# Windowed attention and two MLP layers on one core: block 0's first two steps in column parts, softmax normalising by head, and weight loads behind the third unit's q and k

## The chip, the core and the metric

The kernel runs on one core of a Trainium2 chip. A core has TensorE (PE, matrix multiply), VectorE (DVE), ScalarE (ACT), GpSimd (POOL) and SyncE (SP, which issues all of this kernel's transfers here). The metric is the device time of one execution in microseconds (us); smaller is better.

## What is computed

Attention of 8 heads over 4 batches of 576 tokens with head size 64, then two MLP layers of width 512 and 2048 on all 2304 tokens, in float32.

```python
scores = q @ k.T / 8          # heads 0-3: keys 0..31 positions back
                              # heads 4-7: keys 0..127 positions back, every fourth
scores = where(mask, scores, -1e9); scores -= max
attn = exp(scores); attn /= sum(attn) + 1e-9
x = (attn @ v) with the heads side by side        # 2304 x 512
h = x @ w_in;  g = h * sigmoid(1.702 * h);  x = g @ w_out
h = x @ w_in2; g = relu(h) ** 2;            y = g @ w_out2
```

## The kernel before

**Attention** is cut into units: a batch, a pair of heads and half of the 576 positions, 8 units a batch, 32 in all (`attend`, L407). For heads 4 to 7 the positions are sorted by their remainder by four, so half `u` holds remainders 2u and 2u + 1. A unit works on three blocks of 96 queries by 128 keys for each of its two heads: 12 score matmuls into two PSUM banks (`scores`, L448); six VectorE instructions that add the mask and find the row maxima (L470); six ScalarE exponentials with row sums (L477); a guard and a reciprocal (L491, L494); six instructions that scale 96x128 by the reciprocal, each on ScalarE or VectorE (`normalise`, L496, through `scaled`, L244 and L246); six transposes on TensorE (L527), or from batch 2 on by VectorE (L512); copies into the tile `pt`, of which there is one; 12 value matmuls (L546); then the result is split into a high and a low part, `x` (L240 or L238, and L562). In batch 0 the transposes and values, and the scores of every second unit, use the four PSUM banks of class "o". Units three and six of batch 0 keep their scores in `g` tiles.

**Layers** run over blocks of up to 512 tokens (`BLOCKS1`, `BLOCKS2`). A block has 16 steps `f`, one for each 128 of the 2048 inner columns (`step`, L572). A step does 12 "hidden" matmuls (L590 to L592: four slices `k` of 128 inputs, each as high x high, high x low, low x high), the nonlinearity on ScalarE and VectorE (L613 and L616, or L623 and L626), the split of `g` into `gh` and `gl`, and 12 "output" matmuls (L657 to L659) into four "o" banks that a block holds from its first step to its last. Slice `k` of the inputs is a pair of heads. A block's tokens are ordered by remainder by four, 144 (`ROW`) to a remainder and batch: block 0 has remainders 0, 1 and 2 and 80 tokens of remainder 3 of batch 0. So each of its slices needs both halves of a pair of heads, and block 0 needs all eight units of batch 0, in the order pairs (0, 0, 1, 1, 2, 3, 2, 3), halves (0, 1, 0, 1, 0, 0, 1, 1).

**Weights** come as 64 tiles of 512 KB in eight-byte numbers, and are turned into a high and a low float32r tile by four instructions: a cast of the upper bits, `c` (L238 or L240), a join on VectorE (L314), a high part (L238 or L240) and a low part on VectorE (L249). There are three raw buffers and two `c` buffers. Step `f` needs two weights, (f, 0) for its hidden and (f, 1) for its output matmuls.

**Order.** Every instruction is a task of a planner written into the kernel (`Schedule`, L63). A task has one engine or several to choose from, a cost on each, a due time (`want`), the tasks that it follows and the buffers that it takes. `emit` (L119) again and again takes the task that can start first by its own clock, on ties the one due first, and issues it; so the order on each engine is fixed when the kernel is built. Where GpSimd is among the choices, VectorE is charged 3 us extra for tasks due before 160 us (`spare`). Tasks of GpSimd, and those of VectorE marked `port`, are not placed at the same time. A transfer is ready as soon as its buffer is. While TensorE would idle in batch 0 the planner puts in matmuls on zeros ("warm", L718), which hold one of the two "h" banks until all of batch 0's values are done. Units of batches 1 to 3 are spread between the steps of the first blocks.

Of the kernel before, what the change touches and what calls it, by code (L numbers as in the profile page):

```python
# [15 lines left out]
ALU = mybir.AluOpType  # L16
# [3 lines left out]
P = 128  # L20
# [3 lines left out]
NPAIR = H // 2  # L24
KD = DM // P
KF = DFF // P
WIN = 32
QB = 96
NBLK = 3
# [5 lines left out]
ROW = S // 4  # L35
# [5 lines left out]
A1 = 1.0  # L41
BAND_FROM = 2
W2_GAP = 4.0
WARM = 256
MASK_AT = -9.0
LEAD = (12.0, 8.0, 5.0)
# [21 lines left out]
class Schedule:  # L68
# [18 lines left out]
    def buffer(self, cls):  # L87
        return {"cls": cls, "held": False, "left": 0, "end": 0.0}

    def task(self, engine, cost, want, fn, after=(), bufs=(), port=False):  # L90


        many = isinstance(engine, tuple)
        t = {
            "ways": dict(zip(engine, cost)) if many else {engine: cost}, "many": many,
            "want": want, "fn": fn, "bufs": bufs, "port": port,
            "left": 0, "ready": [], "next": [], "n": len(self.tasks), "end": None,
        }
        for a in after:
            a["next"].append(t)  # L100
            t["left"] += 1
        for b in bufs:
            b["left"] += 1
        self.tasks.append(t)
        return t
# [7 lines left out]

    def open(self, t):
        for e, cost in t["ways"].items():
            ready = max([end + (self.SAME[e] if d == e else self.HOP[d]) for end, d in t["ready"]], default=0.0)
            self.opened[e].append((t, ready, cost, self.spare(t, e)))

    def emit(self):  # L119
# [69 lines left out]
def attention_mlp_mlp(  # L189
# [9 lines left out]
    V, A, G, T = nc.vector, nc.scalar, nc.gpsimd, nc.tensor  # L199
# [89 lines left out]
    def weights(layer, f, part, want):  # L289


        m = {}
        raw_b, c_b, w_b = buffer("raw"), buffer("c"), buffer(f"w{f}_{part}")
        name = f"{f}_{part}"

        def load():

            m["raw"] = wst.tile([P, DM, 2], U32, tag="raw", bufs=RAW_BUFS, name="raw")
            nc.sync.dma_start(
                m["raw"].rearrange("p n t -> p (n t)").bitcast(U16)[:, 0:4 * DM - 1],  # L300
                (w1, w2)[layer][f, part].bitcast(U16)[:, 1:4 * DM],
            )

        def top(e):

            m["c"] = tops[top_count[0] % C_BUFS]
            top_count[0] += 1
            halves = m["raw"].rearrange("p n t -> p (n t)").bitcast(BF16).rearrange("p (n t) -> p n t", t=4)[:, :, 2]  # L310
            copy(e, m["c"].bitcast(F16).rearrange("p (n t) -> p n t", t=2)[:, :, 1], halves)

        def join():
            V.scalar_tensor_tensor(  # L314
                out=m["raw"][:, :, 0], in0=m["raw"][:, :, 0], scalar=13, in1=m["c"],
                op0=ALU.logical_shift_right, op1=ALU.bitwise_or,
            )

        def value():
            return m["raw"][:, :, 0].bitcast(F32)  # L320

        def high_part(e):
            wh[layer, f, part] = wpool.tile([P, DM], F32R, tag="wh" + name, name="wh" + name)
            copy(e, wh[layer, f, part], value())

        def low_part(e):
            wl[layer, f, part] = wpool.tile([P, DM], F32R, tag="wl" + name, name="wl" + name)
            minus(e, wl[layer, f, part], value(), wh[layer, f, part])

        t = task("dma", 1.456, want - LEAD[0], load, (), [raw_b])  # L330
        t = task(("act", "dve"), (0.67, 0.38), want - LEAD[1], top, [t] + tops_zero, [raw_b, c_b], True)
        t = task("dve", 0.602, want - LEAD[1], join, [t], [raw_b, c_b], True)
        hi = task(*copies(DM), want - LEAD[2], high_part, [t], [raw_b, w_b], True)
        lo = task(*pairs(DM), want - LEAD[2], low_part, [hi], [raw_b, w_b], True)
        split_task[layer, f, part] = [hi, lo]
        wbuf[layer, f, part] = w_b
# [70 lines left out]
    def attend(b, p, u, want, start, turn_pe, i):  # L407
# [85 lines left out]
        def recip():  # L493
            V.reciprocal(out=m["st"][:, 2], in_=m["st"][:, 1])  # L494

        def normalise(e, j, i):  # L496
            scaled(e, m["sm", j][:, i], m["sm", j][:, i], m["st"][:, 2, j, i:i + 1])

        es = head(0) + head(1)
        t = task("dve", 0.08, want, guard, es, [st_b], True)  # L500
        t = task("dve", 0.12, want, recip, [t], [st_b], True)
        for j in range(2):
            normal.append([
                task(
                    ("act", "dve"), (0.292, 0.196), want, lambda e, j=j, i=i: normalise(e, j, i),
                    [t], [st_b, sm_bs[j]], True,
                )
                for i in range(NBLK)
            ])

        def band(a, e):
# [41 lines left out]
        for n, w, src_, dst_ in x_pieces(b, p, u):  # L553
            if n not in x_buf:
                x_buf[n] = buffer(x_place[n])

            def to_hi(e, n=n, src_=src_, dst_=dst_):
                copy(e, dst_(x_tile(n), 0), src_(m["o"]))

            def to_lo(n=n, src_=src_, dst_=dst_):  # L560
                x = x_tile(n)
                V.tensor_tensor(out=dst_(x, 1), in0=src_(m["o"]), in1=dst_(x, 0), op=ALU.subtract)  # L562

            t = task(("act", "dve"), (0.07 + w / 1340, dve1(w)), want, to_hi, [pv], [pv_b, x_buf[n]])
            t2 = task("dve", dve1(w), want, to_lo, [t], [pv_b, x_buf[n]])
            x_done.setdefault((n, p), []).extend([t, t2])


    stored = {}
    close = {}  # L570

    def step(layer, blk, f, want, a=0, z=None):  # L572

        z = z or blk["n"]
        n = z - a
# [6 lines left out]
        for k in range(KD):  # L582

            def hidden(k=k):
                if k == 0:
                    m["h"] = bank("h", "h")
                w_hi, w_lo = wh[layer, f, 0], wl[layer, f, 0]
                x = blk["x"]()
                out, ks = m["h"][:, 0:n], slice(k * P, (k + 1) * P)
                T.matmul(out, w_hi[:, ks], x[:, 0, k, a:z], start=(k == 0), stop=False)  # L590
                T.matmul(out, w_hi[:, ks], x[:, 1, k, a:z], start=False, stop=False)  # L591
                T.matmul(out, w_lo[:, ks], x[:, 0, k, a:z], start=False, stop=(k == KD - 1))  # L592

            before = [t] if t else [chain["hidden"]] if "hidden" in chain else []
            t = task(
                "pe", 3 * pe, want + k * 3 * pe, hidden,
                split_task[layer, f, 0] + blk["ready"](k) + before, [h_b, x_b, w_in],
            )
            if k == 0:
                chain["hidden"] = t  # L600
# [37 lines left out]

        hi = task(*copies(n), want, high_part, [last], [g_b, gh_b], True)
        lo = task(*pairs(n), want, low_part, [hi], [g_b, gh_b, gl_b], True)  # L640
        if f == 0:
            blk["o_buf"] = [buffer("o") for _ in range(KD)]
            blk["o"], blk["ost_buf"], blk["evacs"] = {}, {}, {}
        for d in range(KD):


            extra = a > 0
            more_b = [buffer("sshh"[d])] if extra else []

            def project(d=d, extra=extra):  # L650
                if f == 0:
                    blk["o"][d] = bank("o", "o")
                w_hi, w_lo = wh[layer, f, 1], wl[layer, f, 1]
                if extra:
                    m["more", d] = bank("sshh"[d], "more")[:, 0:n]
                out, ds_ = m["more", d] if extra else blk["o"][d][:, a:z], slice(d * P, (d + 1) * P)
                T.matmul(out, w_hi[:, ds_], m["gh"], start=(f == 0 or extra), stop=False)  # L657
                T.matmul(out, w_lo[:, ds_], m["gh"], start=False, stop=False)  # L658
                T.matmul(out, w_hi[:, ds_], m["gl"], start=False, stop=(f == KF - 1))  # L659

            t = task(
                "pe", 3 * pe, want + (12 + 3 * d) * pe, project,
                split_task[layer, f, 1] + [hi, lo], [gh_b, gl_b, w_out, blk["o_buf"][d]] + more_b,
            )
            if f == KF - 1:

                cls = "raw2" if n < blk["n"] and d > 1 else "ost"
# [92 lines left out]
    def step_len(size):  # L760
        return 24 * mm(size)
# [6 lines left out]
    for n, size in enumerate(sizes1):  # L768
        blk = {
            "i": n, "n": size, "c0": sum(sizes1[:n]), "buf": x_buf[n],  # L770
            "x": lambda n=n: x_t[n], "ready": lambda k, n=n: x_done[n, k],
        }
        lb = ((begin + begin2)[n + 1] - begin[n]) / KF
        for f in range(KF):
            step(0, blk, f, begin[n] + lb * f)


# [10 lines left out]
    for n, size in enumerate(BLOCKS2):  # L788
# [2 lines left out]
        cls = ("xx", "x0", "x1", "x2", "xx")[n]  # L791
        blk = {"i": n, "n": size, "c0": c0, "buf": buffer(cls), "done": {}}
        blk["x"] = lambda blk=blk: blk["tile"]
        blk["ready"] = lambda k, blk=blk: blk["done"][k]
        need = [
            i for i, size1 in enumerate(sizes1)
            if sum(sizes1[:i]) < c0 + size and sum(sizes1[:i]) + size1 > c0
# [23 lines left out]
        for f in range(KF):  # L821
            w = want + step_len(size) * f
            if n == len(BLOCKS2) - 1 and f == KF - 1 and size == 512:

                step(1, blk, f, w, 0, size // 2)
                step(1, blk, f, w + step_len(size // 2), size // 2, size)
            else:
                step(1, blk, f, w)

# [87 lines left out]
```

## Time and profile before

| | us |
|---|---|
| median of 3 runs | 891.55 |
| lowest, highest | 890.49, 893.07 |
| the profiled execution | 889.98 |
| its span from first to last instruction | 888.0 |
| TensorE busy in it | 873.6 (98%) |
| VectorE busy | 436.2 (49%) |
| ScalarE busy | 388.3 (44%) |
| GpSimd busy | 2.1 (0%) |

The rows of the profile name an engine, a line of the kernel, an operation, the tile that it writes and the one that it reads, partitions by elements, and how many there are. Busy time is the sum of instructions' durations, which overlap on one engine where it works on several; the distance between starts in the chain of waits tells what one costs in a full queue. "Idle before" names what ended the engine's last wait. The chain of waits goes back from the last instruction and names at each step what released it.

### The profile page before, as it was taken

Reading aid. Unit: us, or ns where it says so; the run is one execution under the profiler, and the core shown is the slowest. Engines: PE = TensorE matmul, PEld = TensorE weight load, DVE = VectorE, ACT = ScalarE, POOL = GpSimd, SP = SyncE. Lnnn points to the kernel's source line nnn. Section 1 sums busy time; section 2 is a strip of 40 time slices with the busy share of each in tenths; the row PEclk is TensorE's granted clock in tenths of the full one; section 3 lists DMA queues with packets and bytes.
Section 4 is the critical chain, followed back from the end, with each engine's and each line's share of the span. In section 5 each row is a group of like instructions: output and inputs, shape, how many; then the busy total and the mean of one; then the engine's idle time right before and its main releaser. Section 6 shows DMA issues by size and latency. Waiting matters only on the chain.

```text
span 888.0 us, 12713 instructions
## 1 busy us (share of the span) xinstructions
PE 873.6 (98%) x4761; PEld 719.9 (81%) x4761; DVE 436.2 (49%) x1231; ACT 388.3 (44%) x1035; POOL 2.1 (0%) x9
## 2 busy tenths in 40 slices
PE   7899999999999999999999999999999999999997
PEld 5677777777799988888877788888889988888886
DVE  6888774666668734446778422422232222222223
ACT  7999976543455523335546322222232322232222
POOL 0000000000000000000000000000000000000000
PEclk9999999999999999999999999999999999999999
DMA  7466752111121100216465200000000000000001
GB/s 253 143 216 205 229 195 87 45 38 42 47 89 58 43 15 1 84 41 220 166 195 186 93 1 1 35 25 1 1 24 25 9 16 1 1 30 18 1 1 48
DMA packets 27533, 64.98 MB, mean 73 GB/s; under 512 B 3056, under 2 KB 9200, under 8 KB 27472
## 3 DMA queue, kind: packets, MB, share of 16 engines
q1 hardware_dynamic: 27472, 64.18, 22.0%
q8 instruction: 37, 0.61, 0.3%
q14 instruction: 24, 0.20, 0.1%
HBM read 54.73 MB, written 9.44 MB: 72 GB/s over the span
## 4 chain that ended last, share of the span: by engine, by line
PE 85%; DVE 5%; DMA 4%; ACT 4%; issue 1%; SPq 0%; DVEq 0%; ACTq 0%
PE o L657 14%; PE h L590 14%; PE o L659 14%; PE o L658 13%; PE h L592 13%; PE h L591 13%; DMA raw<-in_w 3%; PE s L454 2%; PE pv L546 2%; DVE wl L249 1%; ACT sm L477 1%; ACT sm L244 1%; DVE raw L314 1%; PE tp L527 1%; ACT c L238 1%
## 5 line engine op out<-in xcount | busy, mean ns | idle before, releaser
L657 PE MATMUL o<-gh,wh 128*128 128x512 f32 (+1 forms) x640 | 237.3, 371 | 0.3 <-ACT gh L238 0.3
L659 PE MATMUL o<-gl,wh 128*128 128x512 f32 (+1 forms) x640 | 235.7, 368 | 0.6 <-DVE gl L249 0.4
L658 PE MATMUL o<-gh,wl 128*128 128x512 f32 (+1 forms) x640 | 235.1, 367 | 0.0
L590 PE MATMUL h<-x,wh 128*128 128x512 f32 (+1 forms) x512 | 190.9, 373 | 1.9 <-DVE g L616 0.8
L592 PE MATMUL h<-x,wl 128*128 128x512 f32 (+1 forms) x512 | 186.2, 364 | 0.5 <-DVE wl L249 0.5
L591 PE MATMUL h<-x,wh 128*128 128x512 f32 (+1 forms) x512 | 186.0, 363 | 0.1
L626 DVE TENSOR_TENSOR g<-g 128x512 f32<-128x512 f32 (+1 forms) x81 | 51.2, 632 | 217.6 <-ACT g L623 216.8
L623 ACT ACTIVATE g<-h 128x512 f32<-128x512 f32 (+1 forms) x81 | 44.5, 550 | 222.9 <-PE h L592 222.8
L657 PEld LDWEIGHTS o<-gh,wh 128*128 128x128 f32 x640 | 120.6, 188 | 22.8 <-ACT gh L238 1.2
L659 PEld LDWEIGHTS o<-gl,wh 128*128 128x128 f32 x640 | 120.6, 188 | 22.6 <-DVE gl L249 2.6
L658 PEld LDWEIGHTS o<-gh,wl 128*128 128x128 f32 x640 | 120.6, 188 | 19.5
L249 DVE TENSOR_TENSOR gl<-g,gh 128x512 fp32r<-128x512 f32 (+1 forms) x161 | 101.7, 634 | 64.8 <-ACT gh L238 62.2
L238 ACT CAST gh<-g 128x512 fp32r<-128x512 f32 (+1 forms) x149 | 85.9, 580 | 87.3 <-DVE g L626 54.4
L590 PEld LDWEIGHTS h<-x,wh 128*128 128x128 f32 x512 | 96.8, 189 | 20.5 <-DVE g L616 1.8
L592 PEld LDWEIGHTS h<-x,wl 128*128 128x128 f32 x512 | 96.6, 189 | 16.5 <-DVE wl L249 1.2
L591 PEld LDWEIGHTS h<-x,wh 128*128 128x128 f32 x512 | 96.7, 189 | 14.3 <-DVE x L562 0.8
L477 ACT ACTIVATE sm<-sm,st 96x128 f32<-96x128 f32 x180 | 70.1, 393 | 23.6 <-DVE st L470 23.5
L613 ACT ACTIVATE g<-h 128x512 f32<-128x512 f32 (+1 forms) x80 | 43.9, 552 | 77.6 <-PE h L592 75.8
L616 DVE SCALAR_TENSOR_TENSOR g<-g,h 128x512 f32<-128x512 f32 (+1 forms) x80 | 50.2, 629 | 54.1 <-ACT g L613 53.4
L314 DVE SCALAR_TENSOR_TENSOR raw<-raw,c 128x512 uint32<-128x512 uint32 x64 | 44.1, 691 | 21.3 <-ACT c L238 21.0
L238 ACT CAST c<-raw 128x512 f16<-128x512 bf16 x54 | 42.0, 781 | 27.3 <-DMA raw<-in_w 23.7
L470 DVE CUSTOM_DVE_ANT_0 sm<-s,mask_sb 96x128 f32<-96x128 f32 x180 | 41.6, 281 | 24.8 <-PE s L454 23.7
(66 smaller groups left out, 712.8 us busy)
## 6 DMA issues: line engine op xcount, KB each, us to landing
raw<-in_w SPq DMA_DIRECT2D x64, 511.8 KB, 4.0
qk<-in_qkv SPq DMA_DIRECT2D x32, 304.0 KB, 2.9
v<-in_qkv SPq DMA_DIRECT2D x32, 192.0 KB, 2.6
x2d<-ost SPq DMA_DIRECT2D x16, 256.0 KB, 2.2
raw<-x2d SPq DMA_DIRECT2D x16, 256.0 KB, 2.8
out_T<-ost SPq DMA_DIRECT2D x14, 256.0 KB, 2.0
x2d<-ost SPq DMA_DIRECT2D x4, 128.0 KB, 1.7
raw<-x2d SPq DMA_DIRECT2D x4, 128.0 KB, 2.2
```

Source lines behind the costliest of these rows:

```text
L238: A.copy(out, in_)
L249: by_name[e].tensor_tensor(out=out, in0=a, in1=b, op=ALU.subtract)
L314: V.scalar_tensor_tensor(out=m["raw"][:, :, 0], in0=m["raw"][:, :, 0], scalar=13, in1=m["c"], op0=ALU.logical_shift_right, op1=ALU.bitwise_or,
L477: A.activation(out=m["sm", j][:, i], in_=m["sm", j][:, i], func=AF.Exp, bias=m["st"][:, 0, j, i:i + 1], scale=-1.0, accum_out=m["st"][:, 1 ...
L590: T.matmul(out, w_hi[:, ks], x[:, 0, k, a:z], start=(k == 0), stop=False)
L591: T.matmul(out, w_hi[:, ks], x[:, 1, k, a:z], start=False, stop=False)
L592: T.matmul(out, w_lo[:, ks], x[:, 0, k, a:z], start=False, stop=(k == KD - 1))
L616: V.scalar_tensor_tensor(out=g(), in0=g(), scalar=1.0, in1=h(), op0=ALU.add, op1=ALU.mult)
L626: by_name[e].tensor_tensor(out=g(), in0=g(), in1=g(), op=ALU.mult)
L657: T.matmul(out, w_hi[:, ds_], m["gh"], start=(f == 0 or extra), stop=False)
L658: T.matmul(out, w_lo[:, ds_], m["gh"], start=False, stop=False)
L659: T.matmul(out, w_hi[:, ds_], m["gl"], start=False, stop=(f == KF - 1))
```

## The change

Three things. First, a unit's scaling by the reciprocal becomes one task for each head in place of three: one multiplication of 96x384 by the reciprocals, spread along the keys, on GpSimd or VectorE in batch 0, and in later batches the same on VectorE or three instructions on ScalarE. Second, the loads of weights are not ready before 7 us of the planner's clock; before, they were ready at once. Third, the first two steps of block 0 are made in two parts each, columns 0 to 288 (remainders 0 and 1) of both steps, then columns 288 to 512 of both. The first part waits for both halves of pairs 0 and 1 and for the first half alone of pairs 2 and 3, so for the first six units; the second part waits for all. Both parts write the same four "o" banks; only the very first matmul into a bank starts it afresh. Output matmuls of the same part and bank keep the order of steps. Elsewhere in the kernel a step that was already cut in two (the last one) works as before.

```diff
+HALVES = 2
+FIRST = 2 * ROW
+RAW_FROM = 7
...
-    def task(self, engine, cost, want, fn, after=(), bufs=(), port=False):
+    def task(self, engine, cost, want, fn, after=(), bufs=(), port=False, since=0.0):
...
-            ready = max([end + (self.SAME[e] if d == e else self.HOP[d]) for end, d in t["ready"]], default=0.0)
+            ready = max([end + (self.SAME[e] if d == e else self.HOP[d]) for end, d in t["ready"]], default=t["since"])
...
-        t = task("dma", 1.456, want - LEAD[0], load, (), [raw_b])
+        t = task("dma", 1.456, want - LEAD[0], load, (), [raw_b], since=RAW_FROM)
...
-        def normalise(e, j, i):
-            scaled(e, m["sm", j][:, i], m["sm", j][:, i], m["st"][:, 2, j, i:i + 1])
+        def normalise(e, j):
+            if e == "act":
+                for n in range(NBLK):
+                    scaled(e, m["sm", j][:, n], m["sm", j][:, n], m["st"][:, 2, j, n:n + 1])
+            else:
+                by_name[e].tensor_tensor(
+                    out=m["sm", j], in0=m["sm", j],
+                    in1=m["st"][:, 2, j].rearrange("q (i o) -> q i o", o=1).to_broadcast([QB, NBLK, P]),
+                    op=ALU.mult,
+                )
...
         for j in range(2):
+            ways = {"pool": 0.98, "dve": 0.47} if start else {"act": 0.9, "dve": 0.47}
             normal.append([
                 task(
-                    ("act", "dve"), (0.292, 0.196), want, lambda e, j=j, i=i: normalise(e, j, i),
+                    tuple(ways), tuple(ways.values()), want, lambda e, j=j: normalise(e, j),
                     [t], [st_b, sm_bs[j]], True,
                 )
-                for i in range(NBLK)
             ])
...
-            x_done.setdefault((n, p), []).extend([t, t2])
+            x_done.setdefault((n, p, u), []).extend([t, t2])
...
-    def step(layer, blk, f, want, a=0, z=None):
+    def step(layer, blk, f, want, a=0, z=None, own=False):
...
-                split_task[layer, f, 0] + blk["ready"](k) + before, [h_b, x_b, w_in],
+                split_task[layer, f, 0] + blk["ready"](k, z) + before, [h_b, x_b, w_in],
...
-            extra = a > 0
+            extra = own
...
-                if f == 0:
+                if f == 0 and a == 0:
                     blk["o"][d] = bank("o", "o")
...
-                T.matmul(out, w_hi[:, ds_], m["gh"], start=(f == 0 or extra), stop=False)
+                T.matmul(out, w_hi[:, ds_], m["gh"], start=(f == 0 and a == 0 or extra), stop=False)
...
-                split_task[layer, f, 1] + [hi, lo], [gh_b, gl_b, w_out, blk["o_buf"][d]] + more_b,
+                split_task[layer, f, 1] + [hi, lo] + blk.setdefault(("last", a, d), []), [gh_b, gl_b, w_out, blk["o_buf"][d]] + more_b,
             )
+            blk["last", a, d] = [t]
...
-            "x": lambda n=n: x_t[n], "ready": lambda k, n=n: x_done[n, k],
+            "x": lambda n=n: x_t[n],
+            "ready": lambda k, z, n=n: [
+                t for u in range(2) if z > FIRST or k < NPAIR // 2 or u == 0 for t in x_done.get((n, k, u), [])
+            ],
...
-        for f in range(KF):
+        cut = HALVES if n == 0 else 0
+        for i in range(2 * cut):
+            f = i % cut
+            w = begin[n] + (step_len(FIRST) * f if i < cut else step_len(FIRST) * cut + step_len(size - FIRST) * f)
+            step(0, blk, f, w, *((0, FIRST) if i < cut else (FIRST, size)))
+        for f in range(cut, KF):
             step(0, blk, f, begin[n] + lb * f)

```

## Rows read from the trace of the kernel before

**Rows 1.** Stretches: us, busy time and instructions of each engine, clock, DMA share, GB/s

```profile
10.00:47.50 37.50, 33.17 (x305) 22.62 (x303) 31.59 (x174) 37.10 (x155) 0.00 (x0) 1.00 0.57 177
47.50:120.00 72.50, 72.49 (x410) 56.34 (x411) 59.27 (x159) 66.09 (x179) 0.00 (x0) 1.00 0.65 215
120.00:860.00 740.00, 738.20 (x3888) 616.67 (x3887) 333.69 (x856) 273.26 (x673) 0.58 (x1) 1.00 0.16 53
```

**Rows 2.** Order of time, VectorE: start us, us, engine, line, operation

```profile
42.34 0.52 DVE L562 TENSOR_TENSOR x<-pv,x 128x224 fp32r<-128x224 f32 x2
```

**Rows 3.** Order of time, TensorE near 46.5 us; in brackets the idle time before

```profile
46.55 0.50 PE L590 MATMUL h<-x,wh 128*128 128x512 f32 x1 [0.81 <-ACT wh L238]
```

**Rows 4.** Chain of waits, TensorE full: start us, us, line

```profile
59.80 0.83 PE s L454 x12
...
66.99 0.55 PE tp L527 x6
...
68.96 0.65 PE pv L546 x12
...
865.93 0.23 PE h L590
...
874.77 0.11 PE h L590
...
877.64 0.23 PE o L657
```

**Rows 5.** Groups by line and form, 0 to 47.5 us: busy us, mean ns, idle before

```profile
L454 PE MATMUL s<-qk 64*96 64x128 f32 x120 | 11.5, 314 | 3.2 <-DMA qk<-in_qkv 2.2 <-DVE st L470 0.8 <-DVE pt L240 0.2
...
L546 PE MATMUL pv<-pt,v 128*64 128x96 f32 x108 | 8.0, 256 | 0.7 <-ACT pt L238 0.5
```

**Rows 6.** Normalising, 0 to 47.5 us: groups, then order of time, then the chain

```profile
L244 ACT ACTIVATE sm<-sm,st 96x128 f32<-96x128 f32 x28 | 9.0, 400 | 0.2 <-DVE st L494 0.2
...
L246 DVE TENSOR_SCALAR sm<-sm,st 96x128 f32<-96x128 f32 x14 | 3.3, 277 | 0.0
...
L246 DVE TENSOR_SCALAR g<-g,st 96x128 f32<-96x128 f32 x8 | 1.7, 278 | 0.0
...
L244 ACT ACTIVATE g<-g,st 96x128 f32<-96x128 f32 x4 | 1.4, 393 | 0.0
...
41.88 1.89 ACT L244 ACTIVATE sm<-sm,st 96x128 f32<-96x128 f32 x6
...
19.03 0.79 DVE g L246 x4
```

**Rows 7.** Groups of GpSimd, whole span

```profile
L285 POOL MEMSET c<- 128x512 uint32 x2 | 1.0, 524 | 0.3 <-POOLq L900 0.3
...
masks.py:199 POOL TENSOR_SCALAR_AFFINE_SELECT ident<-ident 96x96 f32<-96x96 f32 x1 | 0.3, 262 | 0.1
```

**Rows 8.** Order of time: SyncE's queue and TensorE, and a piece of the chain

```profile
3.52 1.43 SPq L299 DMA_DIRECT2D raw<-in_w  x3
5.35 2.73 SPq L420 DMA_DIRECT2D qk<-in_qkv  x2
...
12.21 0.46 PE L454 MATMUL s<-qk 64*96 64x128 f32 x4 [0.15 <-DMA qk<-in_qkv]
...
2.10 3.94 DMA qk<-in_qkv
```

**Rows 9.** Chain of waits in the block of 256 columns

```profile
295.73 0.34 DVE g L616
...
296.09 0.41 ACT gh L238
```

**Rows 10.** Groups that split weights, 0 to 47.5 us

```profile
L238 ACT CAST c<-raw 128x512 f16<-128x512 bf16 x4 | 3.1, 778 | 0.0
...
L314 DVE SCALAR_TENSOR_TENSOR raw<-raw,c 128x512 uint32<-128x512 uint32 x4 | 2.8, 689 | 1.1 <-ACT c L238 1.1
L249 DVE TENSOR_TENSOR wl<-raw,wh 128x512 fp32r<-128x512 f32 x4 | 2.8, 688 | 0.1
```

## What the change should do to the time

> **What bounds the kernel now.** I read the stretches first [rows 1]. From 47.5 us to the end TensorE is busy without a hole worth the name: 72.49 of 72.50 us, then 738.20 of 740.00, at full clock. So from there the time is a fixed amount of matmul work, and only what TensorE failed to do before can be won. Before it, ScalarE is busy 37.10 of 37.50 us and VectorE 31.59: the attention of batch 0 is bound by these two together. Then the order of time on VectorE and TensorE: the x of the eighth unit is split by 42.34 + 0.52 = 42.86 us [rows 2], and block 0 needs all eight; at 46.55 TensorE ends its last wait of that time, for the high part of a weight [rows 3], and from there it is full.
>
> How much is lost by then? In the chain of waits, where TensorE is full, a unit takes 0.83 + 0.55 + 0.65 = 2.03 us; 39 matmuls of 512 columns lie between 865.93 and 874.77, 0.227 each, and 24 of 256 columns between 874.77 and 877.64, 0.120 each [rows 4]. By 46.55 us TensorE had done the scores of ten units and the transposes and values of nine (120 and 108 matmuls, 12 a unit [rows 5]) and the 24 hidden matmuls of two steps: 10 x 0.83 + 9 x 1.20 + 24 x 0.227 = 24.6 us. So 46.55 - 24.6 = **22.0 us lost**. Everything below asks how large that loss is afterwards; what follows it keeps its length.
>
> **The change, part by part.**
> *Normalising.* Batch 0 has 48 such instructions of 96x128. By 47.5 us the rows count 28 + 4 on ScalarE and 14 + 8 on VectorE; six of those on ScalarE, at 41.88, are the ninth unit's. Back to back one costs 1.89/6 = 0.31 us on ScalarE and 0.79/4 = 0.20 on VectorE [rows 6]. So 26 x 0.31 + 22 x 0.20 = 12.5 us leave the two full engines. They become 16 instructions of 96x384 on GpSimd, which does nothing in this stretch. Their price there is not shown. From below: the memset of 512 columns in 0.52 us gives 0.39 for 384; from above, the select of 96 columns, which reads its input, in 0.26 gives 1.05 [rows 7]. I take 1.05, since this one reads too. 16 x 1.05 = 16.8 us lie beside other work in some 30. On the path only the last unit's pair counts: 2.1 us in sequence, where six instructions took 1.9, so +0.2. Batches 1 to 3 take one VectorE instruction of 384 columns for three of 128, or still three on ScalarE but as one piece of 0.93. TensorE's full rows cover that; without the cover it is worth at most the 1.8 us that TensorE is idle from 120 to 860 us [rows 1], either sign. I put 0.
>
> *Weights behind the third unit's q and k.* On SyncE's queue three weight loads of 512 KB go out at 3.52 us, the third and fourth q/k from 5.35 on; the scores of the third unit wait for that load until 12.21, while the second q/k, with no weights ahead of it, took 3.94 [rows 8]. With the weights held to 7 us of the planner's clock, the third q/k goes at about 5.4 and the scores start near 9.3, some 3 us sooner. Behind the three weight loads now stand the fourth q/k and the next v; they land about as they did. The first cast of a weight comes a microsecond or two later, with the third unit's exponentials to fill ScalarE meanwhile. The two engines are full either way, so this is worth only what of VectorE's idle time it fills: I put 0.2, which the +0.2 above eats.
>
> *Two steps in parts.* Columns 0 to 288 need only the first six units. A part needs tanh, product, high and low part of its own: at 256 columns a product takes 0.34 and a high part 0.41 [rows 9], so I put 0.4 for each of the four, 3.2 us for two steps, ahead of the eighth unit. The two engines so save 12.5 - 3.2 = 9.3 us, half of it in time, 4.65: the eighth unit is split at **38.2** in place of 42.86. On TensorE 48 more matmuls cost 2 x 0.120 - 0.227 = 0.013 each, 0.6 us; per column that makes 0.1335 for 288 and 0.107 for 224. That the weight load lets 224 columns run under the 0.120 of 256 is not shown; if not, 0.6 more.
>
> *The sum.* From 38.2 us TensorE should stay full, as parts of steps are left to do. Lower end: by then it has done eight units and one more's scores (17.1 us), 24 hidden matmuls of 288 columns (3.2) and six of 224 (0.6): 20.9. Lost 17.3, with the 0.6 above 17.9: 22.0 - 17.9 = **4.1 us won**. Upper end: also all output matmuls of the 288 columns (3.2) and twelve more hidden ones of 224 (1.3): **8.6 won**. Between them stand two things. Each output of block 0 takes one of four "o" banks and keeps it for the block, while units seven and eight still need such banks for scores, transposes and values, so not all four outputs can go early. And the second weight of step 0 must be split by then, where weights stand behind attention in the planner's due times. So I take a third of the way: 4.1 + 1.5 = 5.6. The profiled execution has 889.98 us (span 888.0 and 2.0 around it): 884.4. The median of the runs is 1.57 above the profiled one, so **886.0**.
>
> **Rivals.**
> *Better: parts fully overlapped*, 8.6 won, 883.0. For it: GpSimd was idle and the time before 46.55 is bound by the two engines relieved. Against: the banks.
>
> *Weights late.* Three more weights have to be ready by 38 instead of by 46.6. Each costs a cast, a join and a low part, 0.78 + 0.69 + 0.69 [rows 10], and a high part, at least the 0.41 of [rows 9]: 2.6; three are 7.8, over two engines 3.9. If the freed time comes in scraps between units, where no weight fits, TensorE waits for them at 38: 5.6 - 3.9 = 1.7 won, 889.9. For it: the last wait of before is one for a weight. Against: time is freed on just these engines.
>
> *GpSimd and VectorE in each other's way.* The four joins and four low parts of weights on VectorE read two tiles in SBUF, 0.69 us each [rows 10]. GpSimd would be at work half of the time; were such an instruction to wait for a running one of 1.05, that is 0.5 x 0.5 x 1.05 = 0.26 on average, 2.1 us over eight, and about 1 us for GpSimd in return. Half of VectorE's reaches the pace, plus a little: 1.3 less, 4.3 won, 887.3. The trace of before has no GpSimd instruction beside such a one, so it neither shows nor excludes this. (The Trainium skill, page "SBUF — State Buffer", section "Who interferes with whom", says that VectorE instructions with two SBUF inputs hold a port pair that GpSimd's reads need, as copies in a two-port mode do, and that the later one blocks for the whole instruction; by that rule it is this case that comes true, and the forecast is 1.3 us too good. No run here shows it so far.)
>
> *Slower: GpSimd becomes the bound.* Sixteen instructions stand in one queue from about 9.1 us on, and the order on each engine is fixed beforehand, so the transposes on TensorE queue behind a late one, and the next scores and hidden matmuls behind these. At p us each the last ends at 9.1 + 16 p, and some 4 us later the unit is split. With all overlapped work then done (25.4 us, and the 0.6) the loss equals the present one where the split ends at 46.8 us: p = 2.1. From there it decides; at 2.3 the end is 3.1 us later, 894.7. For it: a one-input row scaled up may hide a dearer two-input form. Against: twice the upper bound is needed.
>
> *Not what it says: VectorE gets the normalising.* The planner may choose VectorE for a head: 0.69 x 384/512 = 0.52 each, 8.3 us in all against 12.5, so 4.2 saved, 0.5 in time; the same sum gives -0.1 to 4.4, 1.4 won, 890.2. Against: the planner charges VectorE 3 us extra where GpSimd is an option.
>
> **How the numbers follow.** Forecast 0.40, overlapped 0.10, weights late 0.20, in each other's way 0.15, GpSimd the bound 0.08, VectorE 0.07. The forecast's own range is 4.1 to 7 won, 884.6 to 887.5. Taking in most of the better case, weights late and the port case gives 881.5 to 891.0, with the 1.8 us of idle time and 0.6 of weight loading as margin; left out are GpSimd as the bound and the tails. 0.3%, about what a measurement of this kernel can tell from no change, is 2.7 us: faster means below 888.9. That holds for the forecast, the overlapped case, most of the port case and a third of the two near 890: 0.71. Most of what remains of these is same, 0.19; slower 0.10.
>
> **What would show it.** In the profile after: sixteen GpSimd instructions of about 1 us and no normalising on ScalarE before 40 us; the third unit's scores at 9 to 10 us; the last x of the eighth unit near 38; matmuls of 288 columns ahead of it, some of them outputs; TensorE full from 38 to 39. A GpSimd row of 2 us or more, joins on VectorE that grow past 0.69, or a wait of TensorE on a weight after 38 would make it wrong, in that order of damage.

## The result

The median went from 891.99 us (4 runs, 890.49 to 893.07) to 884.65 us (4 runs, 883.60 to 885.60): a ratio of 0.9919, 95% interval 0.9900 to 0.9938, so 7.3 us faster. The forecast was 886.0, in a range of 881.5 to 891.0, and chance was mostly on faster. The profiled executions differ by less: 889.98 before, 884.82 after (spans 888.0 and 883.0), 5.2 us where the sum said 5.6.

| | before | after |
|---|---|---|
| median | 891.99 | 884.65 |
| profiled execution, span | 889.98, 888.0 | 884.82, 883.0 |
| last part of the eighth unit's x is split | 42.86 | 38.56 |
| TensorE without a hole from (before: but for 0.17 us at 47.45) | 46.55 | 33 |
| third unit's scores begin | 12.21 | 8.76 |
| busy in the span: TensorE, VectorE, ScalarE, GpSimd | 873.6, 436.2, 388.3, 2.1 | 870.5, 429.9, 385.3, 15.4 |

Stretches of the kernel after, to be read against [rows 1]: start and end, us, busy time and instructions of TensorE, of its weight loads, of VectorE, ScalarE and GpSimd, then granted clock, DMA share and GB/s:

```profile
15.00:20.00 5.00, 4.13 (x47) 2.98 (x48) 3.82 (x26) 4.88 (x22) 3.15 (x4) 1.00 0.75 257
...
35.00:40.00 5.00, 5.00 (x48) 4.72 (x48) 4.56 (x22) 5.00 (x19) 0.00 (x0) 1.00 0.70 196
40.00:45.00 5.00, 5.00 (x49) 4.74 (x48) 4.70 (x13) 5.00 (x20) 0.00 (x0) 1.00 0.58 194
...
10.00:47.50 37.50, 35.10 (x354) 28.60 (x353) 33.11 (x169) 36.24 (x153) 12.88 (x16) 1.00 0.73 238
47.50:120.00 72.50, 72.39 (x419) 56.53 (x419) 57.02 (x154) 65.25 (x180) 0.00 (x0) 1.00 0.60 205
120.00:860.00 740.00, 737.77 (x3884) 616.16 (x3882) 328.66 (x816) 272.66 (x657) 0.58 (x1) 1.00 0.16 52
```

From 47.5 us on next to nothing changed: TensorE is busy 72.39 and 737.77 us, 72.49 and 738.20 before, so it idles 0.5 us more. The gain lies ahead of that. TensorE's busy time between 10 and 47.5 us rose from 33.17 to 35.10 us while the warm matmuls in it fell from 21 to 12. ScalarE is still nearly full (36.24 of 37.50), now with weights and the first steps' nonlinearity.

The order of time of the kernel after, several engines (start us, us, engine, line, operation, in brackets the idle time before), to be read against [rows 2, 3, 8]:

```profile
5.16 3.31 SPq L425 DMA_DIRECT2D qk<-in_qkv  x2
8.52 1.38 SPq L304 DMA_DIRECT2D raw<-in_w  x3
...
8.76 1.60 PE L459 MATMUL s<-qk 64*96 64x128 f32 x12
...
9.58 1.61 POOL L506 TENSOR_TENSOR sm<-sm,st 96x384 f32<-96x384 f32 x2 [7.42 <-DVE st L499]
...
10.42 2.29 SPq L425 DMA_DIRECT2D qk<-in_qkv  x2
...
16.82 0.90 PE L459 MATMUL s<-qk 64*96 64x128 f32 x12 [0.27 <-DMA qk<-in_qkv]
...
29.65 0.40 PE L605 MATMUL h<-x,wh 128*128 128x288 f32 x1
...
29.90 3.63 POOL L506 TENSOR_TENSOR sm<-sm,st 96x384 f32<-96x384 f32 x4 [2.02 <-ACT sm L482]
...
30.84 1.22 DVE L254 TENSOR_TENSOR wl<-raw,wh 128x512 fp32r<-128x512 f32 x1
...
37.81 0.38 PE L672 MATMUL o<-gh,wh 128*128 128x288 f32 x1
...
38.04 0.52 DVE L576 TENSOR_TENSOR x<-pv,x 128x224 fp32r<-128x224 f32 x2 [0.41 <-ACT x L243]
...
45.93 0.40 PE L605 MATMUL h<-x,wh 128*128 128x512 f32 x1
```

The queue of SyncE now sends the third and fourth q/k at 5.16, then three weights, then the fifth and sixth q/k. The first hidden matmul of 288 columns starts at 29.65, the first output matmul of that part at 37.81, before the eighth unit's x is done; the first step of 512 columns at 45.93.

Groups by line and form, 0 to 47.5 us, of the kernel after (busy us, mean ns, idle before), to be read against [rows 5, 6, 7, 10]:

```profile
L459 PE MATMUL s<-qk 64*96 64x128 f32 x120 | 11.4, 334 | 2.7 <-DMA qk<-in_qkv 2.7
...
L506 POOL TENSOR_TENSOR sm<-sm,st 96x384 f32<-96x384 f32 x12 | 10.1, 862 | 14.2 <-DVE st L499 11.3 <-ACT sm L482 2.0 <-DVE st L475 0.9
...
L560 PE MATMUL pv<-pt,v 128*64 128x96 f32 x108 | 8.0, 256 | 0.9 <-DVE pt L245 0.3 <-ACT pt L243 0.2
...
L319 DVE SCALAR_TENSOR_TENSOR raw<-raw,c 128x512 uint32<-128x512 uint32 x7 | 4.8, 688 | 0.5 <-ACT c L243 0.5
...
L254 DVE TENSOR_TENSOR wl<-raw,wh 128x512 fp32r<-128x512 f32 x6 | 4.6, 774 | 0.1
...
L506 POOL TENSOR_TENSOR g<-g,st 96x384 f32<-96x384 f32 x4 | 3.2, 824 | 3.8 <-ACT pt L243 2.1 <-DVE st L475 1.8
```

All sixteen multiplications are on GpSimd. The rest of the row tells that it is no bottleneck: it sat idle 14.2 us before twelve of them, most of it waiting for a reciprocal.

### The profile page after: what moved, and what is told of

It is laid out like the page before. It is cut to its first block, busy times and chain, and to the rows that moved or that the text cites. A ratio compares the mean times of both kernels' runs of the same rounds, so it can differ in the third digit from the quotient of the medians.

```text
span 883.0 us, 12736 instructions
## 1 busy us (share of the span) xinstructions
PE 870.5 (99%) x4796; PEld 722.1 (82%) x4796; DVE 429.9 (49%) x1180; ACT 385.3 (44%) x1018; POOL 15.4 (2%) x25
## 4 chain that ended last, share of the span: by engine, by line
PE 81%; DMA 6%; ACT 6%; DVE 5%; issue 1%; SPq 0%; ACTq 0%; DVEq 0%
PE o L672 13%; PE o L674 13%; PE h L605 13%; PE o L673 13%; PE h L607 12%; PE h L606 12%; DMA raw<-in_w 5%; PE s L459 2%; PE pv L560 2%; ACT c L243 1%; DVE wl L254 1%; ACT sm L482 1%; ACT sm L249 1%; ACT wh L243 1%; DVE raw L319 1%
## 5 line engine op out<-in xcount | busy, mean ns | idle before, releaser
L672 PE MATMUL o<-gh,wh 128*128 128x512 f32 (+3 forms) x648 | 239.1, 369 | 0.0
L674 PE MATMUL o<-gl,wh 128*128 128x512 f32 (+3 forms) x648 | 237.4, 366 | 1.6 <-DVE gl L254 1.5
L673 PE MATMUL o<-gh,wl 128*128 128x512 f32 (+3 forms) x648 | 236.6, 365 | 0.0
L605 PE MATMUL h<-x,wh 128*128 128x512 f32 (+3 forms) x520 | 192.0, 369 | 0.7 <-DVE g L631 0.7
L607 PE MATMUL h<-x,wl 128*128 128x512 f32 (+3 forms) x520 | 187.4, 360 | 0.0
L606 PE MATMUL h<-x,wh 128*128 128x512 f32 (+3 forms) x520 | 187.2, 360 | 0.0
L254 DVE TENSOR_TENSOR gl<-g,gh 128x512 fp32r<-128x512 f32 (+3 forms) x163 | 102.3, 628 | 68.6 <-ACT gh L243 66.4
L243 ACT CAST gh<-g 128x512 fp32r<-128x512 f32 (+3 forms) x154 | 88.2, 573 | 93.5 <-DVE g L641 54.4
L631 DVE SCALAR_TENSOR_TENSOR g<-g,h 128x512 f32<-128x512 f32 (+3 forms) x82 | 50.8, 619 | 60.5 <-ACT g L628 59.6
L628 ACT ACTIVATE g<-h 128x512 f32<-128x512 f32 (+3 forms) x82 | 44.6, 544 | 77.6 <-PE h L607 72.7
L606 PE MATMUL h<-xx,wh 128*128 128x512 f32 (+1 forms) x132 | 50.5, 383 | 0.0
```

Of the source, the lines that this page charges most:

```text
L243: A.copy(out, in_)
L254: by_name[e].tensor_tensor(out=out, in0=a, in1=b, op=ALU.subtract)
L631: V.scalar_tensor_tensor(out=g(), in0=g(), scalar=1.0, in1=h(), op0=ALU.add, op1=ALU.mult)
L672: T.matmul(out, w_hi[:, ds_], m["gh"], start=(f == 0 and a == 0 or extra), stop=False)
```

## Experiments

Three theories stood against each other. The prediction's: the two engines relieved of normalising set the pace, the parts fill what opens up, and holding the weights is worth next to nothing. A rival: the parts do nothing, the pace is enough. A second rival: the hold is what matters, because transfers or their order take over once the engines have room. The first experiments undo each part of the change; later ones make a part alone and look into why. Ratios are to the kernel before, run beside them on the same chip; its medians there were 891.83 (the first four experiments), 891.57 (the changed kernel once more, normalising alone, the hold alone, the longer hold with parts) and 891.27 (the rest).

| normalising by head | weights held | parts | median | ratio, 95% |
|---|---|---|---|---|
| yes | yes | yes | 884.65; again 885.46 | 0.9919 (0.9900 to 0.9938); 0.9931 (0.9917 to 0.9946) |
| yes | yes | no | 883.65 | 0.9912 (0.9896 to 0.9927) |
| yes | no | yes | 893.05 | 1.0013 (1.0000 to 1.0025) |
| no | yes | yes | 892.89 | 1.0007 (0.9994 to 1.0020) |
| yes | no | no | 893.84 | 1.0027 (1.0015 to 1.0039) |
| no | yes | no | 892.62 | 1.0015 (1.0006 to 1.0023) |

No run has the parts alone.

**Without the parts.**

```diff
-HALVES = 2
+HALVES = 0
```

> The changed kernel with block 0's first two steps whole again; normalising by head and the held weight loads stay. Theory A (the two full engines set the pace of batch 0, and the 12.5 us of normalising taken off them are the gain): the eighth unit is split near 42.9 - 12.5/2 = 36.6 us and everything behind it moves by as much, so 5 to 6 us under the kernel before (892.0), 886 to 887; the parts are then worth 1.5 to 2.5 of the 7.3. Theory B (the parts carry the gain, since without them TensorE has nothing to do until the eighth unit is split and the weights are ready): 889 to 890, the parts worth 5.

Measured: 883.65 us, as fast as the changed kernel or a little faster, and below the ranges of both theories. Two rows of its order of time, and two stretches:

```profile
18.65 0.90 PE L459 MATMUL s<-qk 64*96 64x128 f32 x12 [1.41 <-DMA qk<-in_qkv]
...
40.11 0.52 DVE L576 TENSOR_TENSOR x<-pv,x 128x224 fp32r<-128x224 f32 x2 [0.44 <-ACT x L243]
```

```profile
35.00:40.00 5.00, 5.00 (x42) 3.72 (x42) 4.06 (x23) 5.00 (x22) 0.33 (x1) 1.00 0.68 224
40.00:45.00 5.00, 4.96 (x34) 3.63 (x32) 4.57 (x11) 5.00 (x15) 0.00 (x0) 1.00 0.65 216
```

The eighth unit is split at 40.63, two microseconds later than with parts, and nothing is lost by that; the fifth unit's scores, too, wait longer here for their q/k. TensorE is busy 5.00 and 4.96 us in 35 to 40 and 40 to 45 us without any part of a step, so the parts had no hole to fill there.

**Without the hold.**

```diff
-RAW_FROM = 7
+RAW_FROM = 0.0
```

> The changed kernel with weight loads ready at once, as before. Theory A: the third unit's scores go back from 8.8 to about 12 us, but ScalarE and VectorE have other work meanwhile; it costs no more than 0.5 us: 884.7 to 885.2. Theory C (the early third unit carries the gain, because without normalising ScalarE would run empty while it waits): 2 to 3 us slower than the changed kernel, 887 to 888, with ScalarE idle 2 us or more between 9 and 13 us.

Measured: 893.05 us, the whole gain gone. Order of time of TensorE, and two stretches:

```profile
13.87 1.55 PE L459 MATMUL s<-qk 64*96 64x128 f32 x24
...
21.10 2.88 PE L459 MATMUL s<-qk 64*96 64x128 f32 x24 [2.71 <-DMA qk<-in_qkv]
```

```profile
15.00:20.00 5.00, 2.39 (x27) 1.44 (x23) 4.87 (x35) 3.96 (x19) 0.00 (x0) 1.00 0.86 288
20.00:25.00 5.00, 3.90 (x29) 3.61 (x30) 1.96 (x14) 3.37 (x17) 1.61 (x2) 0.54 0.53 180
```

The third and fourth unit's scores run together at 13.87, the fifth's wait for a transfer until 21.10, and around that VectorE, now relieved, is busy only 1.96 of 5 us. The last x of the eighth unit is split at 46.53. Theory C had the direction right, but both theories had far less, and C's sign is missing: ScalarE is busy for all of 9 to 13 us, so the loss is made later, at the fifth unit. The granted clock falls to 0.54 there besides. That can't be the bulk of it: over a whole execution the clock is 0.997 in the median of these runs and 0.999 in the changed kernel's, which makes, as an estimate, some 0.002 x 893 = 1.8 us of the 8.

**With the old normalising, hold and parts kept** (and the same with `HALVES = 0`, further down).

```diff
-                    tuple(ways), tuple(ways.values()), want, lambda e, j=j: normalise(e, j),
+                    ("act", "dve"), (0.292, 0.196), want, lambda e, j=j, i=i: old_normalise(e, j, i),
                     [t], [st_b, sm_bs[j]], True,
                 )
+                for i in range(NBLK)
```

> The changed kernel with normalising in instructions of 96x128 on ScalarE or VectorE in all batches, as before. Theory A: the 12.5 us are back on the two engines, 6.2 in time, so about 1 us is left of the gain: 890 to 891.5, the eighth unit split at 43 to 45 us (the parts' extra work is in front of it). Theory B: the parts still give their 4 to 5 us: 887 to 888.

Here `old_normalise` scales one piece of 96x128, as before the change. Measured: 892.89 us; the eighth unit is split at 43.36. So neither the hold nor the parts win any time while ScalarE and VectorE normalise. In the profiled executions the parts do fill a hole here: from 45 to 50 us TensorE is busy 5.00 us, with the hold alone 4.03. But from 120 to 860 us it is busy 736.39 us, with the hold alone 738.42, so what is won is lost again behind; whether the parts cause that, no run shows.

**Old normalising in batches 1 to 3 only**, the same edit under `if not start:`.

> The changed kernel with normalising as before in batches 1 to 3 alone (GpSimd keeps batch 0). All theories: TensorE is full there, so within 1 us of the changed kernel, 883.7 to 885.7. More than 1.5 us either way would say that the later batches are not covered.

Measured: 887.47 us (6 runs, 885.34 to 888.73), ratio 0.9941 (0.9923 to 0.9959). That is 4.4 us under the kernel before, where the changed kernel has 7.3 and 6.1, so the expectation was missed; but the fastest, 885.34, lies inside the changed kernel's own runs (883.34 to 889.49). The profiled execution, 888.31, does not put the loss into the later batches: its eighth unit, of batch 0, is split at 42.44 in place of 38.56, behind a granted clock of 0.50 in 20 to 25 us, and the rest takes 845.9 us, where the changed kernel takes 846.3. What made the other executions longer is not shown, so whether the later batches' normalising is worth 0 or 2 us stays open.

**The changed kernel once more**, as measure for the runs beside it.

> The changed kernel itself, beside the others on one chip, so that they can be compared with it. All theories: 883.6 to 885.6, as in its four runs.

Measured: 885.46 us (6 runs, 883.34 to 889.49). The profiled execution is the slowest, 889.49, and departs from the first one of the same code at the fifth unit's q/k. A row of its chain of waits (start us, us, what), two of its order of time, two stretches:

```profile
10.70 7.78 DMA qk<-in_qkv
```

```profile
18.52 1.60 PE L459 MATMUL s<-qk 64*96 64x128 f32 x12 [1.97 <-DMA qk<-in_qkv]
...
42.97 0.52 DVE L576 TENSOR_TENSOR x<-pv,x 128x224 fp32r<-128x224 f32 x2 [0.39 <-ACT x L243]
```

```profile
15.00:20.00 5.00, 2.56 (x24) 1.97 (x24) 1.80 (x9) 3.03 (x12) 1.61 (x2) 0.84 0.70 246
20.00:25.00 5.00, 4.93 (x37) 3.85 (x36) 3.68 (x27) 3.25 (x16) 1.61 (x2) 0.50 0.39 125
```

The fifth unit's q/k, behind three weights of 512 KB, takes 7.78 us; TensorE is busy 2.56 of 5 us, and then the granted clock is 0.50, the 1.2 GHz level, for all of 20 to 25 us. The eighth unit comes at 43.49 in place of 38.56, and the execution is 889.49 - 884.82 = 4.7 us longer. When the fifth unit's scores start, 1.7 us of that are there (18.52 for 16.82); the rest arises behind, where the clock is low.

**Normalising alone.** `RAW_FROM = 0.0` and `HALVES = 0`.

> Normalising by head alone: weight loads ready at once, block 0's steps whole. Theory A (ScalarE and VectorE set the pace of batch 0): 5 to 6 us under the kernel before, about 886. Theory D (transfers do, once the two engines are relieved: the planner, seeing units go faster, puts a fourth weight load ahead of the fifth unit's q/k, so the engines wait for q and k): no gain, 891 to 894, the fifth unit's scores at 20 us or later and TensorE idle before them for 2 us or more.

Measured: 893.84 us, 2.3 slower than before, although 12.5 us had been taken off the two engines that bound it. Order of time, then a piece of the chain of waits (start us, us, what):

```profile
3.52 1.58 SPq L304 DMA_DIRECT2D raw<-in_w  x3
5.45 3.23 SPq L425 DMA_DIRECT2D qk<-in_qkv  x2
...
14.52 1.55 PE L459 MATMUL s<-qk 64*96 64x128 f32 x24
...
14.82 0.33 SPq L304 DMA_DIRECT2D raw<-in_w  x1
...
20.30 2.49 PE L459 MATMUL s<-qk 64*96 64x128 f32 x24 [1.83 <-DMA qk<-in_qkv]
```

```profile
9.78 0.83 POOL sm L506
...
12.94 1.16 PE pv L560 x12
14.10 0.48 PE tp L541 x3
14.59 0.88 PE s L459 x12
15.47 0.02 issue
15.48 4.78 DMA qk<-in_qkv
```

This is the reason in one chain. Weights go ahead of the third q/k, and in the order built for that the third unit's scores stand on TensorE behind the first unit's values and the second unit's first transposes. The chain leads through these back to the first multiplication on GpSimd, at 9.78. The scores so start at 14.52 (12.21 before), and it is no longer the transfer that holds them: from 13 to 14 us the DMA engines are idle (share 0.00). There are two q/k tiles, so the fifth unit's load can go only when the third unit's scores are done, at 15.48 (13.18 before), and beside the fourth weight it takes 4.78 us; the fifth unit's scores start at 20.30. In the trace of before they start at 16.20. Four microseconds lost there, VectorE busy 2.81 us in 10 to 15 and 2.27 in 20 to 25 (3.93 and 5.00 before), eat what the engines were given. The granted clock is 0.66 in 20 to 25 us besides.

**The hold alone**: `HALVES = 0` with the old normalising.

> Held weight loads alone: normalising as before in all batches, steps whole. Theory A and D: ScalarE and VectorE stay full with normalising, so 890.5 to 892.5, within 0.2% of the kernel before, though the third unit's scores start near 9 us. Theory C (the early third unit is itself the gain): 886 to 888.

Measured: 892.62 us, 1.0 slower than before. Two of its stretches:

```profile
10.00:15.00 5.00, 3.98 (x45) 2.83 (x42) 4.91 (x34) 4.98 (x23) 0.00 (x0) 1.00 0.97 340
15.00:20.00 5.00, 3.59 (x46) 2.75 (x45) 3.43 (x26) 5.00 (x25) 0.00 (x0) 1.00 0.68 229
```

The third unit's scores start at 8.97, three microseconds sooner, and gain nothing: ScalarE is full in both stretches (4.98 and 5.00 of 5 us), and the eighth unit is split at 43.83, later than the 42.86 of before.

**Weights held further**, behind the sixth unit's q/k: `RAW_FROM = 15.0`; and the same without parts.

> The changed kernel with weight loads held to 15 us of the planner's clock in place of 7: by the order on SyncE's queue the first three then stand behind the sixth unit's q/k in place of the fourth's. Theory D: the fifth unit's scores start near 13 to 14 us in place of 16.8, and ScalarE and VectorE are no longer short of work between 14 and 18: 1 to 3 us faster than the changed kernel, 881.5 to 883.5. Theory A: those engines were nearly full there anyway and the weights come later: 884 to 886.

> Steps of block 0 whole and the weight loads held to 15 us, normalising as in the changed kernel. Theory D with parts worth nothing: the fifth unit's scores near 14 to 15 us, 882 to 884.5. If the weights then come too late for the first whole step: 885 to 888, with TensorE waiting on a weight's part between 30 and 40 us.

Measured: 885.11 us (0.9924, 0.9908 to 0.9940) and 885.31 us (0.9933, 0.9918 to 0.9947). Order of time of the first:

```profile
14.91 0.90 PE L459 MATMUL s<-qk 64*96 64x128 f32 x12
...
27.02 0.90 PE L459 MATMUL s<-qk 64*96 64x128 f32 x12 [0.96 <-DMA qk<-in_qkv]
```

The fifth unit's scores start at 14.91 without a wait, but the wait comes back at a later unit, behind the weights that are now loaded there (0.95 of the DMA engines' time is taken in 20 to 25 us). Holding longer moves the collision and wins nothing more. The second run lies in the range of late weights, but for another reason: from 25 to 50 us TensorE waits for `pt` (1.4 us in all) and for no weight.

**Only the fourth weight and those after it held**, the first three ahead of the third q/k as before; on the normalising alone.

```diff
-        t = task("dma", 1.456, want - LEAD[0], load, (), [raw_b], since=RAW_FROM)
+        t = task("dma", 1.456, want - LEAD[0], load, (), [raw_b], since=0.0 if layer == 0 and f + 1.5 * part < 2 else 20.0)
```

> Normalising by head alone, as in the run that had only that (893.8), but with the fourth and later weight loads not ready before 20 us of the planner's clock; the first three go out early, as before. On SyncE's queue the fourth then stands behind the eighth unit's q/k. Theory D1 (it is the fourth load, ahead of the fifth unit's q/k, that costs most): the fifth unit's scores start at 16 to 17.5 us in place of 20.3, and 4 to 7 us come back: 887 to 890. Theory D2 (the first three, ahead of the third unit's q/k, cost it all): 892 to 894.

Measured: 891.28 us, 1.0000 (0.9988 to 1.0012), between the two theories. The fifth unit's scores start at 18.89 in place of 20.30, since no weight goes out beside its q/k; the third's still only at 14.47. Against the kernel before, normalising alone is 2.3 us slower, this run as fast, and normalising with the full hold 8.2 us faster. So of these 10.4 us the fourth load accounts for some 2.3, the first three with the order of work that follows from them for some 8.2. No run separates those three transfers from that order.

**Normalising by head on VectorE in batch 0.**

```diff
-            ways = {"pool": 0.98, "dve": 0.47} if start else {"act": 0.9, "dve": 0.47}
+            ways = {"dve": 0.47} if start else {"act": 0.9, "dve": 0.47}
```

> The changed kernel with batch 0's normalising by head on VectorE, none on GpSimd. Theory A (what counts is the work taken off both engines): 16 x about 0.45 us on VectorE in place of 12.5 us on both, so 5 us are saved instead of 12.5 and VectorE becomes the fuller one: 887.5 to 890. Theory E (taking it off ScalarE is enough, GpSimd is not needed): 884 to 886.5.

Measured: 892.94 us, 1.0016 (1.0004 to 1.0027), outside both ranges. The rival of the prediction for this case had 890.2. Two rows of TensorE's order of time:

```profile
42.80 0.40 PE L605 MATMUL h<-x,wh 128*128 128x288 f32 x1 [0.19 <-ACT wh L243]
...
43.53 0.40 PE L607 MATMUL h<-x,wl 128*128 128x288 f32 x1 [0.19 <-DVE wl L254]
```

The eighth unit is split at 41.81, a microsecond before the 42.86 of the kernel before, yet nothing is won: the high and the low tile of the weight for the second step come only after it, and no hidden matmul runs between 35.1 and 42.80. So in this trace the time is lost where ScalarE and VectorE split weights, and not in the units. The granted clock was 0.66 and 0.65 in 15 to 25 us, so this trace doesn't say how much each costs.

**GpSimd's price tripled**, order unchanged: two more multiplications into a scratch tile ahead of each.

> The changed kernel with GpSimd's price tripled: each multiplication is done twice more into a scratch tile first, with the planner told nothing, so the order is the same. The sixteen then take 2.4 us each, above the 2.1 at which the prediction put the break-even. By its formula the last one ends at 9.6 + 16 x 2.43 = 48.5 us and the eighth unit is split 4 us later: 5 to 7 us slower than the kernel before, 897 to 899. If instead the gaps between units (GpSimd is busy 13 of 24 us) take up part of it, 889 to 893.

Measured: 909.32 us, 1.0198 (1.0183 to 1.0212), 10 to 12 us beyond what the formula of the prediction gave. The waits of TensorE up to 60 us (total, times, longest), two rows of GpSimd in order of time, and a stretch:

```profile
PE tp L548 <- POOL sm L513: 13.2, 10, 2.4
```

```profile
33.97 1.73 POOL L508 TENSOR_TENSOR scratch<-sm,st 96x384 f32<-96x384 f32 x2 [3.00 <-DVE st L500]
...
56.95 1.16 POOL L513 TENSOR_TENSOR sm<-sm,st 96x384 f32<-96x384 f32 x1
```

```profile
30.00:35.00 5.00, 3.97 (x33) 3.25 (x35) 2.38 (x13) 2.02 (x11) 1.85 (x4) 0.50 0.24 68
```

The transposes wait 13.2 us for GpSimd in ten places, as that rival said. But the last multiplication ends at 58.1, not at 9.6 + 16 x 2.43 = 48.5, nor at the 51.0 that follows from the 2.59 us that three take from start to start: GpSimd itself sat idle (3.00 us here, 2.27 once more) for reciprocals that come late because TensorE had queued behind GpSimd, and at 0.50, the lower level of the clock, TensorE was slow besides.

## Why the prediction came out right, and what in it was wrong

**The bound, and where the loss lies: right.** After 47.5 us nothing moved. By 45.93 us TensorE had done the scores of ten units, transposes and values of nine, 24 hidden and 24 output matmuls of 288 columns, 24 hidden and 12 output matmuls of 224. Put into matmuls of 512 at 0.227 where both parts are done, and 12 outputs of 288 by their columns: 8.3 + 10.8 + 36 x 0.227 + 12 x 0.128 = 28.8 us. So 17.1 us are lost, where 22.0 were: 4.9 of the profiled 5.2. The forecast had 16.4.

**The eighth unit at 38.2: the number right (38.56), by luck; its derivation not.** "The two engines so save 9.3 us, half of it in time" gives, without the parts' 3.2 us, 42.86 - 6.25 = 36.6. The kernel without parts has 40.63, normalising alone 47.83, both where the rule says 36.6. Relieving two full engines is worth half the saving only while nothing else comes due, and here a transfer and the order that goes with it came due at once.

**Weights behind the third q and k at 0.2: the step that failed.** Its mechanism was seen: the scores at 9.3 in the forecast, 8.76 in the trace. Its worth was read from the kernel before, where "the two engines are full either way"; the hold alone confirms that, 1.0 us slower. With the engines relieved it decides everything: 893.05 without it, 893.84 without it and the parts, against 884.65 and 883.65. I costed each edit against the old bound, and the sum of edits made alone is +2.3 + 1.0, while together, without parts, they give -8.2. That the total came out near is luck in part: the sum took for granted that transfers and their order keep pace, put the hold, which sees to that, at 0.2, and gave the parts a worth that no run shows.

**Two steps in parts: their price seen, their worth wrong.** The four operations on 288 columns take about 0.45 us each (the product 445 ns, the low part 449), those on 224 columns 0.38, so 0.41 on average where 0.4 stood. On TensorE 12 matmuls of 224 columns take from 44.59 to 45.93, 0.112 each, and one of 288 0.1325, so 0.017 more a pair in place of 0.013; 224 columns do run under 0.120. The upper half of the 4.1 to 8.6 was put down to the parts, but kernels with parts, less those without, each against the kernel before that ran beside it, give +0.8 and +2.1 (all three parts of the change), 0.0 (old normalising), -1.1 (no hold) and -0.5 us (longer hold). Of a gain near 1.5 to 4.5 us, which the forecast and its upper end rested on, nothing is to be seen; whether it is one or minus one stays open. The cap by the "o" banks was not met: all four outputs of the first 288 columns were made by 39.9 us, TensorE had been full since 33.

**GpSimd's price: right side, too high.** An undisturbed pair takes 1.61 us, 0.81 each, within 0.39 to 1.05 and under the 1.05 taken. (The Trainium skill, page "GPSIMD Engine Reference", section "3.1 Elementwise — side-by-side cycle accounting", gives 4497 ns for a two-input operation of 2048 columns; scaled to 384 that is an estimate of 0.84, and the trace agrees.)

**Rivals.** *In each other's way* happens, but seldom: of six low parts of weights one took 1.22 us beside GpSimd's row at 29.90, the others 0.68 to 0.69, and the joins kept their 688 ns [rows 10]; GpSimd's four there took 3.63 in place of 3.24. That is 0.5 us on VectorE, not 2.1. (By the Trainium skill, page "SBUF — State Buffer", section "Who interferes with whom", whichever of the two is later blocks while the other holds the ports they share. The trace agrees in kind: the low part starts at 30.84, inside GpSimd's row, and is the longer one. The prediction's 1.3 us it doesn't bear out, as the planner keeps most such tasks apart.) *Weights late* did not happen in the changed kernel, though it did with the normalising on VectorE. From 40 us to the end TensorE's only waits are these, and none is for a weight:

```profile
PE o L674 <- DVE gl L254: 1.5, 3, 0.7
PE h L605 <- DVE g L631: 0.7, 3, 0.3
```

*GpSimd the bound*: right in mechanism, too mild in price. At 2.43 us each the formula leads to 897 to 899, and 909.3 was measured; the tasks behind GpSimd's feed GpSimd again. *VectorE gets it*: 2.7 us too good. The eighth unit is earlier than it said (41.81, where a saving of 0.5 gives 42.4), but late weights come with it, which it left out.

**The signs.** One of them failed: ScalarE normalises before 40 us, six instructions at 36.66 and 37.88, the ninth unit's, which comes earlier than before. The others were seen: the sixteen on GpSimd, the third unit's scores (8.76, a little ahead of the 9 to 10), outputs ahead of the eighth unit's x, TensorE full from 38 us.

**From the profile to the median.** I added 1.57 us for the median of before over its profiled run. After's median is 0.17 below its profiled execution, 1.74 lower than I had put it, while the profiled execution came out 0.42 above the sum (884.82 for 884.4). So this term, the mis-sized one, makes the 1.35 us by which the forecast was too high.

## What to carry to other kernels

Price an edit that looks free ("the engines are full anyway") again on the kernel that the other edits leave behind: here two edits that each cost 1 to 2 us when made alone won 8.2 together. When an engine is relieved, follow the next unit's input back through its queue, its buffers and the instruction that frees them; a load that goes out when an earlier unit is read turns one late unit into a late chain. And undo each part of a change by itself: the largest part of this diff brought nothing measurable.

## What the runs showed of the hardware

One late transfer can cost twice, once as a wait and, in some executions, once in TensorE's clock. In the changed kernel's second profile TensorE was busy 2.56 of 5 us before the fifth unit's q/k came, and in the next 5 us the granted clock was 0.50; the same code without the late transfer had 4.13 busy in that stretch, kept 1.00 and was 4.7 us shorter. The same drop stands in the kernel without the hold (0.54 after 2.39 us of work in 5). It doesn't always follow: without the parts TensorE was busy 3.11 of 5 us there, with a wait of 1.41, and kept 1.00, while with the old normalising in later batches 3.13, with a wait of 1.39, were followed by 0.50. What decides between these two, and why the same q/k load takes 7.78 us in one execution and has landed within 6.4 in another, is not settled by these runs.
